# Attention and two MLPs on one core: normalising four units at their output, and masking eight on TensorE

## The chip, the cores and the metric

One core of a Trainium2 chip runs the whole kernel as one program. The metric is device time in microseconds, the median of the runs, lower is better. TensorE multiplies matrices (its weight loads are listed apart), VectorE and ScalarE do elementwise work, GpSimd does elementwise work that stays out of PSUM, and SyncE issues most transfers.

## The reference

For 4 batches, 8 heads, 576 positions and 64 columns per head: causal attention with a "forget" bias, then two MLPs over the 2304 rows of 512 columns.

```python
scores = scale * np.matmul(q, k.transpose(0, 1, 3, 2))
causal = np.triu(np.ones((S, S), dtype=bool), k=1)
cum = np.cumsum(np.maximum(s, 0.0), axis=-1)
bias = -(cum[:, :, :, None] - cum[:, :, None, :])
scores = np.where(causal, -1000000000.0, scores + np.minimum(bias, 0.0))
attn = np.exp(scores - np.max(scores, axis=-1, keepdims=True))
attn = attn / (np.sum(attn, axis=-1, keepdims=True) + 1e-09)
x = np.matmul(attn, v)            # heads side by side: (2304, 512)
h = np.maximum(x @ w_in, 0.0); x = (s * (h * h) + b) @ w_out          # first MLP
h = x @ w_in2; out = (np.maximum(h, 0.0) + alpha * np.minimum(h, 0.0)) @ w_out2
```

The weights arrive as 64-bit floats and are converted in the kernel.

## The kernel before

Attention is cut into 32 units. A unit is one batch, one pair of heads and one of two ranges of query rows: rows 0 to 320 in three blocks (64, 128 and 128 rows), or rows 320 to 576 in two blocks of 128. Units 0 to 3 are the first range of batch 0, units 4 to 7 its second range. `EARLY` is 4: these units have buffers of their own, in the room of weights that come later. `NATIVE` is 8: these units multiply in plain float32, the others in split halves.

For each head of a unit, `scores` first makes the bias of each block in an SBUF tile (L431 on ScalarE or L435 on VectorE) and has GpSimd put the mask on the diagonal square (`affine_select`, L439). TensorE multiplies queries and keys (L457); VectorE adds scores and bias and keeps the row extreme (L461); ScalarE takes the exponential with a running sum in `sm` (L473); VectorE adds 1e-9 and takes the reciprocal (L480, L481); GpSimd multiplies each block of probabilities by it (L484). `values` then transposes the probabilities on TensorE into two PSUM banks (L515), copies them out (L519), multiplies them with the values (L531) and copies the result into the MLP's input `xf` (L546). Heads follow each other as interleaved generators: `values` of one runs beside `scores` of a later one. Four PSUM buffers `b` serve scores and transposes, and single banks `hp`, `av` and `acc_first` the rest.

`busy` puts filler products of 512 bfloat16 columns (L97) into TensorE's queue in program order while the units 0 to 3 run. The first MLP works on blocks of 256 rows; its first block needs units 0 to 3, and its matmuls (L772 up, L886 down) are interleaved with later units at a pace set by `pace`. Weight packets are fetched on SyncE's queue and converted on ScalarE, VectorE and GpSimd (L140 to L142, L130, L131), four packets ahead. The order of instructions on each engine is not the written one: the program is built with `schedule_with_timeline_sim=True`, and a planner takes, for each engine, what is ready by its own costs, first written first. A tile's buffer is given out again when its last reader is done.

Of the kernel before, what the change touches and what calls it, by code (L numbers as in the profile page):

```python
# [8 lines left out]
F32 = mybir.dt.float32  # L9
# [10 lines left out]
def tile_forget_attention__then__two_mlps(  # L20
# [20 lines left out]
    nc = tc.nc  # L41
# [11 lines left out]
    R1 = IB[2][1]  # L53
    QK = S - R1 + S
    EARLY, NATIVE = NP, 2 * NP

# [20 lines left out]
    nc.sync.dma_start(out=gates, in_=s.rearrange("b h t -> (b h) t"))  # L79
    ident = const.tile([P, P], F32, name="ident")  # L80
    make_identity(nc, ident)
    misc = const.tile([P, 24], F32, name="misc")
    nc.vector.memset(misc[:, 23:24], 0.0)
    nc.scalar.activation(misc[:, 23:24], misc[:, 23:24], AF.Exp)
# [193 lines left out]
    class Unit:  # L278
        def __init__(self, n):
            self.n = n  # L280
            self.b, self.pr, self.rng = units[n]
            self.tag = "_".join(str(i) for i in units[n])
            self.h0 = 2 * self.pr
            self.blocks = (0, 1, 2) if self.rng == 0 else (3, 4)
            self.q0, self.q1 = (0, R1) if self.rng == 0 else (R1, S)
            self.nv = 3 if self.rng == 0 else 4
            self.probs = [None, None]

            self.early = 0 < n < EARLY
            self.native = n < NATIVE  # L290
            self.n_banks = 0
            self.cums = []
# [111 lines left out]
    def scores(u, h):  # L404

        own = HALF[h]
        head = u.b * H + u.h0 + h
        flip = u.native and h == 1
        nr = len(u.blocks)
        nm = two.tile([P, 3], F32, tag="nm", name=f"nm_{u.tag}_{h}")  # L410
        sm = two.tile([P, 3], F32, tag="sm", name=f"sm_{u.tag}_{h}")
        if u.rng == 0:
            nc.gpsimd.memset(sm[:, 0:1], 1.0)
        big = None if u.early else two.tile([P, 1088], F32, tag="probs", name=f"probs_{u.tag}_{h}")
        probs, col = {}, 0
        for r in u.blocks:
            i0, i1 = IB[r]
            rows = i1 - i0
            if u.early and r != 1:
                big, col = u.buf(two, 0, F32, "", f"probs{h}{r}"), 0  # L420

            width = -(-i1 // P) * P if i1 < S else S
            pt = probs[r] = big[:, col : col + width]
            col += width
            if width > i1:
                nc.gpsimd.memset(pt[:, i1:], 0.0)
            if r == 0:
                nc.gpsimd.memset(pt[64:P, 0:64], 0.0)

            if flip:  # L430
                nc.scalar.activation(  # L431
                    pt[:rows, :i1], u.cums[h][:rows, :i1], AF.Relu, scale=-1.0, bias=cumT[:rows, r, head : head + 1]
                )
            else:
                nc.vector.tensor_scalar(  # L435
                    out=pt[:rows, :i1], in0=u.cums[h][:rows, :i1], scalar1=cumT[:rows, r, head : head + 1],
                    scalar2=0.0, op0=ALU.subtract, op1=ALU.min,
                )
            nc.gpsimd.affine_select(  # L439
                out=pt[:rows, i0:i1], in_=pt[:rows, i0:i1], pattern=[[-1, rows]], base=0,  # L440
                channel_multiplier=1, compare_op=ALU.is_ge,
                fill=-MASKED if flip else MASKED,
            )
        u.probs[h] = probs
        for m, r in enumerate(u.blocks):
            i0, i1 = IB[r]
            rows, n = i1 - i0, i1
            a0 = i0 - u.q0
            pt = probs[r]
            init = -KEEP_ALL if flip else KEEP_ALL  # L450
            for j0, j1 in ([(0, n)] if n <= 512 else [(0, 320), (320, n)]):
                sc = u.bank("sc", f"sc{h}_{r}_{j0}")

                scr, all_ = sc[:rows, : j1 - j0], sc[:, : j1 - j0]
                aq = slice(a0, a0 + P)
                if u.native:
                    nc.tensor.matmul(all_, u.qk[0][own, aq], u.qk[1][own, j0:j1], start=True, stop=True)  # L457
                else:
                    nc.tensor.matmul(all_, u.xs[h][0][:, aq], u.xs[h][1][:, j0:j1], start=True, stop=False)  # L459
                    nc.tensor.matmul(all_, u.ql[h][:, aq], u.xs[h][1][:, j0:j1], start=False, stop=True)  # L460
                nc.vector.tensor_tensor_reduce(  # L461
                    out=pt[:rows, j0:j1], in0=scr, in1=pt[:rows, j0:j1], scale=SCALE if flip else -SCALE, scalar=init,
                    op0=ALU.subtract if flip else ALU.add, op1=ALU.max if flip else ALU.min,
                    accum_out=nm[:rows, m : m + 1],
                )
                if u.n < EARLY:
                    busy(1)
                init = nm[:rows, m : m + 1]
            if flip:
                nc.vector.tensor_scalar(  # L470
                    out=nm[:rows, m : m + 1], in0=nm[:rows, m : m + 1], scalar1=-1.0, scalar2=None, op0=ALU.mult
                )
            nc.scalar.activation(  # L473
                pt[:rows, :n], pt[:rows, :n], AF.Exp, bias=nm[:rows, m : m + 1], scale=1.0 if flip else -1.0,
                accum_out=sm[:rows, m : m + 1],
            )
            yield
        if u.n == 0:
            busy(4)
        nc.vector.tensor_scalar(out=sm[:, :nr], in0=sm[:, :nr], scalar1=1e-9, scalar2=None, op0=ALU.add)  # L480
        nc.vector.reciprocal(sm[:, :nr], sm[:, :nr])  # L481
        for m, r in enumerate(u.blocks):
            rows, n = IB[r][1] - IB[r][0], IB[r][1]
            nc.gpsimd.tensor_scalar(  # L484
                out=probs[r][:rows, :n], in0=probs[r][:rows, :n], scalar1=sm[:rows, m : m + 1],
                scalar2=1.0, op0=ALU.mult, op1=ALU.mult,
            )
        yield

    def values(u, h):  # L490
# [10 lines left out]
        for n_bank, bank in enumerate(banks):  # L501
            f0, fn = bank[0][1], bank[-1][1] + width[bank[-1][0]]
            tp = u.bank("tr", f"pt{h}_{n_bank}")
            moves = []
            for c, off in bank:
                for r in u.blocks:
                    i0, i1 = IB[r]
                    if P * c >= i1:
                        continue

                    partial = r and P * c > i0
                    o = off + i0 - max(q0, P * c)
                    moves.append((not partial, -c if partial else o, o, r, min(P * c, S - P)))
            for _, _, o, r, k0 in sorted(moves):
                nc.tensor.transpose(tp[:, o : o + P], u.probs[h][r][:, k0 : k0 + P], ident)  # L515
            n_p = (2 * h + n_bank) % 2
            if u.native:
                pf = two.tile([P, 512], F32, tag=("ph", "pl")[n_p], name=f"pf_{u.tag}_{h}_{n_bank}")
                (nc.scalar.copy, nc.vector.tensor_copy)[n_p](pf[:, f0:fn], tp[:, f0:fn])  # L519
                parts = (pf,)  # L520
            else:
                ph = two.tile([P, 512], F32R, tag="ph", name=f"ph_{u.tag}_{h}_{n_bank}")
                pl = two.tile([P, 512], F32R, tag="pl", name=f"pl_{u.tag}_{h}_{n_bank}")
                split(ph[:, f0:fn], pl[:, f0:fn], tp[:, f0:fn])
                parts = (ph, pl)
            yield
            for z, part in enumerate(parts):
                for c, o in bank:
                    w = width[c]
                    lhs = (u.vn if u.native else u.vs[h])[:, c].rearrange("p z d -> p (z d)")  # L530
                    nc.tensor.matmul(  # L531
                        av[:, nq - w : nq], lhs, part[:, o : o + w],
                        start=(c == 0 and z == 0), stop=(c == last_c and z == len(parts) - 1),
                        skip_group_check=True,
                    )
        if u.n < EARLY:
            busy(4 if (u.n, h) == (EARLY - 1, 0) else 1)
        t0 = u.b * S + q0
        while t0 < u.b * S + q1:
            t = t0 // T  # L540
            t1 = min((t + 1) * T, u.b * S + q1)
            a = t0 - u.b * S - q0
            cols = slice(a, a + t1 - t0)
            dst, src = x_block(t)[own, u.pr, t0 - t * T : t1 - t * T], av[own, cols]
            if u.native:
                nc.scalar.copy(dst, src)  # L546
            else:
                nc.scalar.copy(dst, av[HALF[1 - h], cols])
                nc.vector.tensor_tensor(out=dst, in0=src, in1=dst, op=ALU.add)
            t0 = t1  # L550
# [490 lines left out]
```

## Time and profile before

| | us |
|---|---|
| median of 3 runs | 1040.58 (1040.21 to 1042.25) |
| the profiled execution, its own time | 1043.1 |
| its span in the trace | 1041.2 |
| TensorE busy | 1021.4 (98% of the span) |
| VectorE, ScalarE, GpSimd busy | 686.3, 672.7, 468.1 |

Times are measured from the start of the span. The busy time of TensorE has modelled ends, so two of its instructions can overlap in the list; the distance from one start to the next is the safer measure. The granted clock is the share of 2.4 GHz that TensorE had.

### The profile page before, as it was taken

How to read it: one execution, taken by the hardware profiler on the slowest of the kernel's cores; microseconds unless marked ns; L12 is line 12 of the kernel's file. 1: busy time of each engine (PE TensorE's matmuls, PEld its weight loads, DVE VectorE, ACT ScalarE, POOL GpSimd, SP SyncE). 2: the span in 40 equal slices, each digit the busy share in tenths (PEclk: the TensorE clock that was granted, in tenths of full speed). 3: DMA queues.
4: the chain of work that ended last, by engine and by line, in shares of the span. 5: the costliest groups of instructions: out<-in, count | busy, mean ns of one | idle time of the engine just before them, and what ended most of it. 6: DMA issues, size and time to landing. Idle time of an engine off the chain costs nothing.

```text
span 1041.2 us, 20629 instructions
## 1 busy us (share of the span) xinstructions
PE 1021.4 (98%) x6952; PEld 927.0 (89%) x6952; DVE 686.3 (66%) x1605; ACT 672.7 (65%) x1669; POOL 468.1 (45%) x892
## 2 busy tenths in 40 slices
PE   9889999999999999999999999999999999999998
PEld 4568899999999999999999888998799999999996
DVE  6879875687677766667655975767775456446443
ACT  5868866777787877778776776645564455345443
POOL 5546675666677666677562100288721011001000
PEclk9889999999999999999999999999999999999999
DMA  7979533343232432234214762466654235334331
GB/s 157 268 174 252 150 63 69 69 97 72 52 84 62 90 92 52 67 68 93 64 44 145 241 201 81 124 194 200 196 178 143 98 101 179 105 95 132 107 104 55
DMA packets 197929, 125.44 MB, mean 120 GB/s; under 512 B 138496, under 2 KB 167936, under 8 KB 197824
## 3 DMA queue, kind: packets, MB, share of 16 engines
q1 hardware_dynamic: 193744, 123.56, 42.9%
q8 instruction: 55, 0.90, 0.4%
q10 hardware_dynamic: 4080, 0.57, 0.3%
q14 instruction: 50, 0.41, 0.1%
HBM read 106.19 MB, written 17.90 MB: 119 GB/s over the span
## 4 chain that ended last, share of the span: by engine, by line
PE 77%; DMA 5%; POOL 5%; ACT 4%; DVE 4%; issue 3%; SPq 1%; ACTq 0%; DVEq 0%; POOLq 0%
PE hp L772 18%; PE acc L896 16%; PE acc L886 16%; PE p L806 13%; PE pt L515 4%; PE av L531 4%; POOL sum L727 2%; PE sc L460 2%; DMA vn<-in_v_dram 1%; PE sc L459 1%; DMA sums_d<-w 1%; DMA wo<-in_moe_w_out_dram 1%; PE acc_first L97 1%; PE sc L457 1%; POOL probs L484 1%
## 5 line engine op out<-in xcount | busy, mean ns | idle before, releaser
L772 PE MATMUL hp<-xh,w 128*128 128x256 f32 (+1 forms) x1024 | 229.1, 301 | 0.5 <-ACT r L791 0.5
L896 PE MATMUL acc<-w,ring 128*128 128x512 f32 x864 | 214.1, 391 | 0.0
L896 PEld LDWEIGHTS acc<-w,ring 128*128 128x128 f32 x864 | 156.0, 188 | 27.8
L772 PEld LDWEIGHTS hp<-xh,w 128*128 128x128 f32 x1024 | 171.4, 189 | 6.6 <-ACT r L791 1.0
L886 PE MATMUL acc<-gh,w 128*128 128x256 f32 x896 | 172.3, 286 | 0.5 <-ACT res L915 0.3
L772 PE MATMUL hp<-xl,w 128*128 128x256 f32 (+1 forms) x512 | 152.6, 298 | 0.0
L886 PEld LDWEIGHTS acc<-gh,w 128*128 128x128 f32 x896 | 136.0, 189 | 3.1 <-issue 1.6
L872 POOL TENSOR_TENSOR cc<-u,t 128x256 f32<-128x256 f32 x32 | 25.9, 809 | 228.9 <-DVE u L863 198.9
L886 PE MATMUL acc<-gl,w 128*128 128x256 f32 x448 | 118.7, 288 | 2.0 <-POOL gl L131 2.0
L484 POOL TENSOR_SCALAR probs<-probs,sm 64x64 f32<-64x64 f32 (+4 forms) x160 | 91.0, 581 | 64.8 <-DVE sm L481 52.5
L473 ACT ACTIVATE probs<-probs,nm 64x64 f32<-64x64 f32 (+4 forms) x160 | 90.0, 563 | 37.8 <-DVE nm L461 25.7
L131 POOL TENSOR_TENSOR gl<-r,gh 128x256 fp32r<-128x256 f32 x112 | 89.3, 797 | 51.3 <-ACT gh L130 44.8
L806 PE MATMUL p<-xs,sums 128*128 128x256 f32 x768 | 104.4, 282 | 0.7 <-DVE u L848 0.7
L806 PEld LDWEIGHTS p<-xs,sums 128*128 128x128 f32 x768 | 97.8, 189 | 2.8 <-DVE u L848 1.2
L772 PEld LDWEIGHTS hp<-xl,w 128*128 128x128 f32 x512 | 97.1, 190 | 3.3 <-issue 0.4
L461 DVE CUSTOM_DVE_ANT_0 probs<-sc,probs 128x320 f32<-128x320 f32 (+3 forms) x160 | 68.2, 427 | 40.4 <-PE sc L460 28.0
L791 ACT ACTIVATE r<-hp 128x256 f32<-128x256 f32 (+1 forms) x144 | 58.1, 403 | 44.5 <-PE hp L772 36.9
L806 PEld LDWEIGHTS p<-xs,w 128*128 128x128 f32 x576 | 78.8, 189 | 9.0 <-DVE u L863 2.3
L806 PE MATMUL p<-xs,w 128*128 128x256 f32 x576 | 82.2, 283 | 2.4 <-DVE u L863 1.5
L886 PEld LDWEIGHTS acc<-gl,w 128*128 128x128 f32 x448 | 80.1, 189 | 4.8 <-POOL gl L131 2.6
L515 PE MATMUL pt<-ident,probs 128*128 128x128 f32 x480 | 75.0, 277 | 5.7 <-POOL probs L484 5.6
L817 DVE SCALAR_TENSOR_TENSOR ph<-pl,misc,ph 128x512 f32<-128x512 f32 x64 | 52.7, 823 | 38.2 <-ACT pl L833 38.0
(149 smaller groups left out, 2133.9 us busy)
## 6 DMA issues: line engine op xcount, KB each, us to landing
sums<-sums_d SPq DMA_DIRECT2D x128, 256.0 KB, 2.7
wi<-in_moe_w_in_dram SPq DMA_DIRECT2D x32, 512.0 KB, 5.0
wo<-in_moe_w_out_dram SPq DMA_DIRECT2D x32, 512.0 KB, 5.0
cum<-cum_d SPq DMA_DIRECT2D x32, 288.0 KB, 3.8
sums_d<-w SPq DMA_DIRECT2D x64, 128.0 KB, 1.9
cum<-cum_d SPq DMA_DIRECT2D x30, 160.0 KB, 3.2
nat<-in_k_dram SPq DMA_DIRECT2D x64, 72.0 KB, 2.5
x_d<-res SPq DMA_DIRECT2D x18, 256.0 KB, 2.2
```

The costliest lines, as they stand in the source:

```text
L131: lo_eng.tensor_tensor(out=lo, in0=src, in1=hi.bitcast(F32), op=ALU.subtract)
L461: nc.vector.tensor_tensor_reduce(out=pt[:rows, j0:j1], in0=scr, in1=pt[:rows, j0:j1], scale=SCALE if flip else -SCALE, scalar=init, op0=AL ...
L473: nc.scalar.activation(pt[:rows, :n], pt[:rows, :n], AF.Exp, bias=nm[:rows, m : m + 1], scale=1.0 if flip else -1.0, accum_out=sm[:rows, m ...
L484: nc.gpsimd.tensor_scalar(out=probs[r][:rows, :n], in0=probs[r][:rows, :n], scalar1=sm[:rows, m : m + 1], scalar2=1.0, op0=ALU.mult, op1=A ...
L515: nc.tensor.transpose(tp[:, o : o + P], u.probs[h][r][:, k0 : k0 + P], ident)
L531: nc.tensor.matmul(av[:, nq - w : nq], lhs, part[:, o : o + w], start=(c == 0 and z == 0), stop=(c == last_c and z == len(parts) - 1), ski ...
L772: nc.tensor.matmul(hs, a[:, c], b[c], start=(n == 0), stop=(n == len(terms) * NCC - 1))
L791: relus.append(nc.scalar.activation(r, hs, AF.Relu, scale=1.0 / W_SCALE).ins)
L806: nc.tensor.matmul(bank, lhs[:, c * P : (c + 1) * P], rhs[:, c], start=(start and c == 0 and z == 0), stop=(c == 1 and z == 2), skip_group ...
L817: nc.vector.scalar_tensor_tensor(out=r, in0=u, scalar=nalpha[:, f : f + 1], in1=r, op0=ALU.mult, op1=ALU.add).ins
L886: nc.tensor.matmul(banks[d] if count == 2 else acc[d // 2][:, d % 2], a[:, d * P : (d + 1) * P], b, start=(f == 0 and (d % 2 == 0 or count ...
L896: nc.tensor.matmul(banks[m], a[:, m * P : (m + 1) * P], b, start=(f == 0 and b is woh and a is gh), stop=(f == NF - 1 and a is gl),)
```

## The change

For units 0 to 3 (`LATE_SCALE`) the probabilities are not normalised. They are transposed and multiplied as the exponentials left them. The reciprocals of each block are then spread by TensorE over all partitions (a float32 product of a broadcast column with the identity) into the free end of the second transposed bank; ScalarE copies that spread into `xf`, where it had copied the result, and VectorE multiplies the result by it. For units 0 to 7 (`MASK_PE`) GpSimd's selection on the bias tile goes; TensorE adds the mask to the scores in PSUM, as one product of a bfloat16 identity with a bfloat16 mask for each block. Two constant tiles are made at the start.

```diff
+    LATE_SCALE = 4
+    MASK_PE = 8
...
+    one_mask = [const.tile([P, P], BF16, name=f"one_mask{z}") for z in range(2)]
+    causal = two.tile([P, T], F32, tag="r", name="causal")[:, :P]
+    nc.gpsimd.memset(causal, 0.0)
+    nc.gpsimd.affine_select(
+        out=causal, in_=causal, pattern=[[-1, P]], base=0, channel_multiplier=1, compare_op=ALU.is_ge, fill=MASKED
+    )
+    nc.scalar.copy(one_mask[0], ident)
+    nc.scalar.copy(one_mask[1], causal)
...
+            if u.n < MASK_PE:
+                continue
             nc.gpsimd.affine_select(
                 out=pt[:rows, i0:i1], in_=pt[:rows, i0:i1], pattern=[[-1, rows]], base=0,
...
                 if u.native:
+                    masked = u.n < MASK_PE and j1 == i1
                     nc.tensor.matmul(all_, u.qk[0][own, aq], u.qk[1][own, j0:j1], start=True, stop=True)
+                    if masked:
+                        nc.tensor.matmul(
+                            sc[:, i0 - j0 : i1 - j0], one_mask[0], one_mask[1][:, :rows], start=False, stop=True,
+                            skip_group_check=True,
+                        )
...
         nc.vector.reciprocal(sm[:, :nr], sm[:, :nr])
+        u.sums[h] = sm
         for m, r in enumerate(u.blocks):
+            if u.n < LATE_SCALE:
+                break
             rows, n = IB[r][1] - IB[r][0], IB[r][1]
             nc.gpsimd.tensor_scalar(
...
+        late = u.n < LATE_SCALE
+        if late:
+            spread = tp[:, 512 - nq :] if u.rng == 0 else u.bank("sc", f"spread{h}")[:, :nq]
+            for m, r in enumerate(u.blocks):
+                i0, i1 = IB[r]
+                nc.tensor.matmul(
+                    spread[:, i0 - q0 : i1 - q0],
+                    u.sums[h][: i1 - i0, m : m + 1].to_broadcast([i1 - i0, P]),
+                    ident[: i1 - i0, : i1 - i0], start=True, stop=True, skip_group_check=True,
+                )
...
-            if u.native:
+            if late:
+                nc.scalar.copy(dst, spread[own, cols])
+                nc.vector.tensor_tensor(out=dst, in0=src, in1=dst, op=ALU.mult)
+            elif u.native:
                 nc.scalar.copy(dst, src)
```

## Rows read from the trace of the kernel before

**Rows 1.** Busy us by stretch; then granted clock, DMA share, GB/s.

```profile
36.30:43.10 6.80, 6.80 (x19) 4.19 (x19) 5.35 (x18) 6.10 (x19) 3.00 (x7) 0.50 0.89 209
...
53.40:60.20 6.80, 4.50 (x14) 3.08 (x15) 4.59 (x15) 3.03 (x8) 5.49 (x9) 0.50 0.97 194
...
8.50:64.13 55.63, 49.58 (x203) 28.64 (x201) 44.84 (x154) 38.92 (x114) 29.44 (x68) 0.88 0.91 234
64.13:140.00 75.87, 74.57 (x498) 63.49 (x497) 67.45 (x139) 60.66 (x146) 49.81 (x73) 1.00 0.66 166
140.00:1041.00 901.00, 890.05 (x6235) 831.73 (x6233) 570.81 (x1307) 571.61 (x1409) 382.66 (x707) 1.00 0.39 110
```

**Rows 2.** Waits of TensorE, 8.50 to 64.13: us, times, longest.

```profile
PE pt L515 <- POOL probs L484: 4.9, 4, 2.8
```

**Rows 3.** TensorE in order of time: start, us, instruction.

```profile
33.12 1.05 PE L515 MATMUL pt<-ident,probs 128*128 128x128 f32 x6 [1.13 <-POOL probs L484]
...
55.70 0.90 PE L515 MATMUL pt<-ident,probs 128*128 128x128 f32 x3 [2.79 <-POOL probs L484]
...
64.13 0.47 PE L772 MATMUL hp<-xh,w 128*128 128x256 f32 x1
```

**Rows 4.** ScalarE in order of time.

```profile
10.15 0.35 ACT L473 ACTIVATE probs<-probs,nm 64x64 f32<-64x64 f32 x1 [7.47 <-DMA natk<-in_k_dram]
...
37.28 0.34 ACT L473 ACTIVATE probs<-probs,nm 64x64 f32<-64x64 f32 x1
...
40.46 0.55 ACT L473 ACTIVATE probs<-probs,nm 128x320 f32<-128x320 f32 x1
...
44.84 0.35 ACT L473 ACTIVATE probs<-probs,nm 64x64 f32<-64x64 f32 x1
...
49.02 0.19 ACT L473 ACTIVATION_READ_ACCUMULATOR probs<-probs,nm 128x1 f32 x1
```

**Rows 5.** VectorE in order of time.

```profile
32.95 0.90 DVE L141 TENSOR_SCALAR wt<-wt 128x512 uint32<-128x512 uint32 x1 [0.67 <-ACT wt L140]
...
39.50 0.42 DVE L141 TENSOR_SCALAR wt<-wt 128x512 uint32<-128x512 uint32 x1
...
41.52 0.40 DVE L131 TENSOR_TENSOR xl<-xf,xh 128x256 fp32r<-128x256 f32 x1
43.48 0.22 DVE L519 COPY pf<-pt 128x64 f32<-128x64 f32 x1 [1.56 <-PE pt L515]
...
53.54 0.25 DVE L480 TENSOR_SCALAR sm<-sm 128x3 f32<-128x3 f32 x1
...
54.30 0.16 DVE L481 RECIPROCAL sm<-sm 128x3 f32<-128x3 f32 x1
```

**Rows 6.** Busy time of GpSimd's line 484 in the first stretch.

```profile
8.50:64.13 55.63, 13.00 (x26) 0.88 0.91 234
```

**Rows 7.** TensorE in order of time: distances between starts.

```profile
9.20 0.59 PE L457 MATMUL sc<-turned 64*128 64x192 f32 x2
9.72 0.39 PE L97 MATMUL acc_first<-dense 128*128 128x512 bf16 x1
...
10.78 1.25 PE L97 MATMUL acc_first<-dense 128*128 128x512 bf16 x5
11.96 0.43 PE L457 MATMUL sc<-turned 64*128 64x64 f32 x2
...
15.99 0.82 PE L515 MATMUL pt<-ident,probs 128*128 128x128 f32 x6
16.74 0.59 PE L457 MATMUL sc<-turnedk,turnedq 64*128 64x192 f32 x2
...
26.07 0.33 PE L531 MATMUL av<-pf,vn 128*128 128x64 f32 x2
26.24 0.59 PE L97 MATMUL acc_first<-dense 128*128 128x512 bf16 x2
```

**Rows 8.** Busy time of GpSimd's line 439 in the first stretch.

```profile
8.50:64.13 55.63, 9.60 (x28) 0.88 0.91 234
```

More of the change, by code (lines that the diff above doesn't have):

```diff
@@ L287, in __init__ @@
             self.probs = [None, None]
+            self.sums = [None, None]
             self.early = 0 < n < EARLY
```

## The prediction

> **What bounds the kernel now.** I read the busy times by stretch first. From 140 us to the end TensorE is busy 890.05 of 901.00 us at the full clock, and from 64.13 to 140 it is busy 74.57 of 75.87 [rows 1]. Nothing else counts there: the kernel ends when TensorE has done its list. The first stretch is different. Between 8.50, where the first scores start, and 64.13, where the first MLP matmul starts (last row of [rows 3]), TensorE is busy 49.58 of 55.63 us, and its mean granted clock is 0.88 [rows 1]. So the time is a ledger of TensorE: its work, plus its idle time, plus what it loses at the low clock. The change can take from the last two in the first stretch only, and it adds to the first.
>
> What can be taken? The waits of TensorE in that stretch have one large entry: transposes of probabilities (L515) that waited for GpSimd's normalisation (L484), four times, 4.9 us together and 2.8 us the longest [rows 2]. The list of TensorE shows two: 1.13 us before the transpose at 33.12, and 2.79 before that at 55.70 [rows 3]. What lies behind the second is seen on three engines. ScalarE had the last exponential and its sum done at 49.02 + 0.19 = 49.2 [rows 4]; VectorE took up the sum only at 53.54, behind other work in its queue, and the reciprocal at 54.30 [rows 5]; GpSimd multiplied after that. The transpose could have run 6 us earlier had it needed only the exponentials.
>
> Then the clock. In 36.30 to 43.10 and 53.40 to 60.20 the granted clock is 0.50 (1.2 GHz) [rows 1]; the mean of 0.88 says that the rest of the stretch ran at 2.4 GHz (13.6 x 0.5 / 55.63 = 0.12). The first begins 3 us after the wait that ends at 33.12, the second inside the one that ends at 55.70 [rows 3]. TensorE is busy 6.80 us in the first and 4.50 us in the second; at the full clock the same work takes half of it, so 3.40 + 2.25 = 5.65 us are lost.
>
> **The change part by part.**
>
> *Normalisation of units 0 to 3.* GpSimd loses 24 of the 26 multiplications of L484, which take 13.00 us together [rows 6]. In their place the transposes follow the exponentials directly, and the 4.9 us of waits [rows 2] go. I take all 4.9, since each of the four waits names that line. The lower bound is 0, where the transpose then waits for something else just as late.
>
> *The clock.* If those waits go, I take it that both low stretches go: −5.65 us. The other end is 0: the clock falls somewhere all the same.
>
> *Spreads.* Per head three fp32 products of 64, 128 and 128 columns, 24 in all, each of two passes. Nothing like them is in the trace, so I bound them by start-to-start distances [rows 7]. Two passes of 64 columns inside a run of value products: 26.07 to 26.24, 0.17 us. Six one-pass transposes of 128 columns: 15.99 to 16.74, 0.125 each, hence 0.25 for two passes. A head is then 0.17 + 0.25 + 0.25 = 0.67 us, and eight heads 5.4 us. The upper end is a lone score product between fillers, two passes of 192 columns from 9.20 to 9.72: 0.52 x 24 = 12.5 us; the lower is the 64-column price for all, 0.17 x 24 = 4.1. I take 5.4, since the spreads stand in a row behind value products.
>
> *Masks on TensorE.* 40 bfloat16 products of 128 columns: 28 in the first stretch (24 of units 0 to 3, 4 of unit 4, whose scores run there), 12 after it. The filler of 512 columns in a run of five takes (11.96 − 10.78) / 5 = 0.236 us [rows 7]; a quarter is 0.06, so 40 x 0.06 = 2.4 us. The upper end adds what changing between kinds of product costs: the lone pair of 192 columns took 0.52, of which its columns at the transposes' rate are 0.125 x 1.5 x 2 = 0.375, so 0.145 for coming and going, and 40 x 0.205 = 8.2. I take 2.4, since the mask stands where a filler or another score product would have paid that change anyway. The Trainium skill, "TensorE: Matmul & The Clock Gate", section on the back-to-back issue gap, speaks against the cheap price: it gives some 81 ns for a matmul of 128 columns in a stream, which would make the masks 3.2 us and the whole sum 0.8 worse. The same section gives 131 ns for 512 columns, and there the trace has 236, so I keep to the row.
>
> *GpSimd's masks.* 28 selections of L439 take 9.60 us in the first stretch [rows 8]; all go there, and 12 later. No wait of TensorE in [rows 2] names them: 0. What hides them is that bias tiles are ready before the scores. One fill and one selection more at the start lie in GpSimd's first microseconds.
>
> *VectorE.* It gets 16 multiplications in place of nothing, 256 or 64 columns: by a subtraction of 256 columns at 41.52 (0.40) and a copy of 64 at 43.48 (0.22) [rows 5], 8 x 0.62 = 5.0 us. It gets back what GpSimd held up: the same 512-column shift takes 0.90 at 32.95 beside L484 and 0.42 at 39.50 without [rows 5]; one hit for each of eight groups is 8 x 0.48 = 3.8. Net +1.2, and VectorE is busy 44.84 of 55.63 there [rows 1]: taken as 0, and 1.2 if that room is gone. The last multiplication stands before the first MLP block: VectorE's 0.62 against what TensorE has left of unit 4 to transpose, 0.3 taken, 0 to 0.7.
>
> *ScalarE.* The 16 copies out of PSUM stay (another source). Two copies of 128 columns are new; each is under the 0.55 of a 320-column exponential, and ScalarE has nothing until 10.15, where it ends 7.47 us of waiting for a load [rows 4]: 0.
>
> *Waits that are added.* The tile of sums (`sm`, two buffers) lives until the spread has read it, so the exponentials of the head after next wait for the spread; behind them on ScalarE stand weight conversions. The transposed bank is held until ScalarE has copied the spread, and one bank (`hp`) serves every second transposition. I take 0, since the transposes come earlier by what L484 and its wait took; the price if not is a rival below.
>
> **Sum.** −4.9 − 5.65 + 5.4 + 2.4 + 0.3 = −2.45 us. The profiled execution took 1043.1 (span 1041.2), so 1040.65 in its own time. The median of the three runs is 1040.58, 2.5 under the profiled one; on that scale the forecast is 1038.1.
>
> **The rivals.** *(a) The clock is won back once only.* Another wait keeps one low stretch, some 2.8 us: −2.45 + 2.8 = +0.4, 1041.0. For it: TensorE has 6.05 idle us in the first stretch, and 1.1 of them are not L484's. Against: fillers cover most of it.
>
> *(b) The spread becomes the wait; slower.* Place: the exponentials of unit 3, first head, at 37.28 [rows 4]. They would need the spread of unit 2, first head, which follows the copy of its last transposed columns at 43.48 + 0.22 [rows 5] by 0.67: 44.4, so 7.1 us late if those transposes come no earlier. From the last of these exponentials (40.46 + 0.55) to the first of the second head (44.84) there are 3.8 us of slack, so 3.3 pass on, and the first low stretch stays (3.40): −2.45 + 3.3 + 3.4 = +4.3, 1044.8. It decides once that exponential starts later than about 41 on the old time scale. For it: the old order has that copy late. Against: it was late because of the wait for GpSimd and the low clock, which both stand before it.
>
> *(c) The products are dear.* At the upper ends: −10.55 + 12.5 + 8.2 + 0.3 = +10.45, 1051.0; half way from the forecast, +4.0, 1044.6. For it: before 29 us TensorE shows no gaps, so what is added there is paid in full.
>
> *(d) More is won than the ledger lists*, since the transposes come 6 us earlier in the last unit and the planner lays out the first stretch afresh: twice the forecast, −4.9, 1035.7.
>
> **How the numbers follow.** A change under 0.2% (2.1 us) can't be told from none here. The forecast case, with its own range from −4.5 to −0.5, has 0.47 (0.34 faster, 0.13 within); (a) 0.20 (within 0.18, slower 0.02); (b) 0.15 and (c) 0.10, all slower but 0.01; (d) 0.08, all faster. Faster 0.42, within 0.32, slower 0.26. The range leaves a tenth at each side: down to (d) and a little over it, up to (b) and the half-way (c): 1035 to 1045.
>
> **What would show it.** Right: no wait of TensorE for L484 before the first MLP matmul; granted clock 1.00 from 8.5 us on; that matmul at about 60.7 (64.13 − 4.9 − 5.65 + 5.4 + 28 x 0.06); spreads at 0.17 to 0.25 start to start; TensorE dense after it. Wrong: low stretches that stay or move; ScalarE's exponentials waiting for TensorE; spreads at 0.5 us; the first MLP block stopped by VectorE's multiplication or by weights, which would mean that the ledger of TensorE is not the whole time.

## The result and the profile after

The changed kernel takes 1046.37 us (median of 12 runs, 1044.22 to 1052.22), the kernel before 1040.74 beside it; the ratio is 1.0055, with a 95% interval of 1.0042 to 1.0067. The change costs 5.6 us. Forecast were 1038.1 and a range of 1035 to 1045, so the time lies above it.

Each run also tells its span and mean granted clock. TensorE at 1.2 GHz does half of what it does at 2.4 GHz: in the kernel before, four fillers in a row start 0.43 us apart at 41.05, where the granted clock is 0.50, and 0.22 us apart at 46.79, where it is 1.00.

```profile
41.05 1.91 PE L97 MATMUL acc_first<-dense 128*128 128x512 bf16 x4
...
46.79 1.03 PE L97 MATMUL acc_first<-dense 128*128 128x512 bf16 x4
```

So for a kernel in which TensorE is nearly always busy, span times mean clock is about the span that the run would have had at the full clock. It is used below as "span at full clock" (the clock has three digits, so one run is good to some 0.5 us). The medians, those of the kernel before from its largest set of runs, beside e9 to e12:

| | time | mean clock | span | span at full clock | time outside the span |
|---|---|---|---|---|---|
| before | 1040.87 (29 runs) | 0.996 | 1038.8 | 1034.0 | 1.98 |
| after | 1046.37 (12 runs) | 0.998 | 1043.7 | 1041.2 | 2.63 |

So the span at full clock, TensorE's list with its idle time, grew by 7.2 us, the clock gave back 2.3 (4.8 lost before, 2.5 after), and 0.65 lies outside the span. The three make the 5.6.

The profiled execution of the changed kernel is the slowest of its twelve (1052.22, mean clock 0.991). The rows by stretch, with the columns of [rows 1]:

```profile
11.00:21.20 10.20, 9.98 (x28) 4.39 (x28) 2.17 (x11) 2.04 (x8) 0.00 (x0) 0.50 0.69 175
8.50:68.60 60.10, 57.13 (x272) 34.78 (x277) 43.02 (x166) 39.47 (x115) 9.46 (x20) 0.91 0.84 220
68.60:140.00 71.40, 69.83 (x464) 59.23 (x462) 65.19 (x135) 58.23 (x137) 43.94 (x57) 0.98 0.65 171
140.00:1049.00 909.00, 896.73 (x6281) 838.76 (x6279) 571.82 (x1317) 574.01 (x1416) 387.04 (x711) 1.00 0.39 109
```

Against [rows 1] the first MLP matmul comes at 68.60 instead of 64.13, 4.5 us later. GpSimd is down from 29.44 to 9.46 us there, VectorE from 44.84 to 43.02. TensorE is busy 57.13 of 60.10 us. The two low stretches of before are gone; this execution has another at 11.0 to 21.2, where TensorE is busy 9.98 of 10.20 us. From the first MLP matmul to the end it takes 980.9 us instead of 977.1; two low stretches of 3.4 us, which cost half of their length, are nearly all of that.

The waits of TensorE in that stretch, which answer to [rows 2]:

```profile
PE sc L471 <- DVE sm L499: 1.6, 1, 1.6
PE pt L537 <- POOL probs L506: 0.6, 1, 0.6
PE sc L471 <- DVE turned L386: 0.5, 1, 0.5
PE acc_first L553 <- DVE pf L541: 0.3, 1, 0.3
PE acc_first L107 <- issue: 0.2, 1, 0.2
```

The 4.9 us for GpSimd's normalisation are gone (the 0.6 is unit 4, which still has it, at L506 now). Of other waits there are 2.6 us, where the kernel before had 1.1. The longest ends at 55.30. TensorE's list shows it, and masks and a head's spreads as well:

```profile
9.62 0.23 PE L473 MATMUL sc<-one_mask,one_mask 128*128 128x128 bf16 x1
9.69 0.38 PE L107 MATMUL acc_first<-dense 128*128 128x512 bf16 x1
...
40.66 1.07 PE L563 MATMUL pt<-ident,sm 64*128 64x64 f32 x6
41.56 0.59 PE L107 MATMUL acc_first<-dense 128*128 128x512 bf16 x2
...
52.50 1.25 PE L537 MATMUL pt<-ident,probs 128*128 128x128 f32 x10
55.30 1.02 PE L471 MATMUL sc<-turned 64*128 64x448 f32 x2 [1.55 <-DVE sm L499]
```

The mask at 9.62 costs 0.07 from start to start, where 0.06 was forecast. The six spread passes of a head cost 0.90 at 40.66, and 0.98 in the mean, where 0.67 was forecast. What the wait at 55.30 was for is seen on VectorE, whose list before it is:

```profile
53.76 0.54 DVE L579 TENSOR_TENSOR xf<-acc_first,xf 64x256 f32<-64x256 f32 x2
54.23 1.02 DVE L386 STREAM_TRANSPOSE turned<-nat 128x832 f32<-128x832 f32 x1
55.18 0.12 DVE L499 TENSOR_SCALAR sm<-sm 128x3 f32<-128x3 f32 x1
```

The view puts the wait down to L499, which ended last; the scores read nothing of it. The scores of unit 4 needed its turned queries and keys (L386, until 55.25), which stood behind two of the new multiplications (L579), and these behind weight conversions. VectorE's queue is what is late next.

And ScalarE shows the wait that rival (b) spoke of, an exponential that waits for a spread to release the tile of sums:

```profile
50.62 0.46 ACT L492 ACTIVATE probs<-probs,nm 128x192 f32<-128x192 f32 x1 [0.94 <-PE pt L563]
```

For a ledger of TensorE up to the first MLP matmul, each instruction is charged the distance to the next start, less the idle time between; half of what falls into a low stretch is put down to the clock (us, profiled executions):

| | fillers | scores | masks | transposes | spreads | values | other | idle | low clock | start | sum |
|---|---|---|---|---|---|---|---|---|---|---|---|
| before | 16.84 | 16.69 | 0 | 7.19 | 0 | 8.82 | 1.55 | 6.05 | 5.67 | 1.31 | 64.13 |
| after | 14.30 | 16.98 | 2.26 | 6.67 | 7.85 | 9.12 | 1.62 | 3.48 | 5.01 | 1.31 | 68.60 |

Not all of the 2.5 us less for fillers is real. The program has the same 59 in both kernels, but five are missing from the trace of the changed one, and their time is booked beside them. Another 0.7 us is the start: the last of the first sixteen fillers starts at 6.7 us in one execution and at 5.9 in the other. Up to 5.6 and 4.2 us they start 0.43 us apart, although the granted clock reads 1.00 there.

### The profile page after: what moved, and what is told of

Same layout as the page of the kernel before. It is cut to its first block, busy times and chain, and to the rows that moved or that the text cites. A ratio compares the mean times of both kernels' runs of the same rounds, so it can differ in the third digit from the quotient of the medians.

```text
span 1049.5 us, 20739 instructions
## 1 busy us (share of the span) xinstructions
PE 1030.4 (98%) x7035; PEld 935.8 (89%) x7040; DVE 683.5 (65%) x1621; ACT 673.8 (64%) x1671; POOL 447.5 (43%) x830
## 4 chain that ended last, share of the span: by engine, by line
PE 84%; DVE 4%; ACT 3%; DMA 3%; POOL 3%; issue 2%; SPq 0%; ACTq 0%; DVEq 0%; POOLq 0%
PE hp L807 20%; PE acc L921 18%; PE acc L931 17%; PE p L841 13%; PE av L553 5%; PE pt L537 4%; PE sc L471 2%; PE sc L479 2%; PE sc L478 2%; DMA sums_d<-w 1%; POOL sum L762 1%; PE acc_first L107 1%; DVE probs L446 1%; PE colsum L255 1%; DMA vn<-in_v_dram 1%
## 5 line engine op out<-in xcount | busy, mean ns | idle before, releaser
L492 ACT ACTIVATE probs<-probs,nm 128x192 f32<-128x192 f32 (+4 forms) x160 | 90.0, 562 | 42.5 <-DVE nm L480 23.5
L506 POOL TENSOR_SCALAR probs<-probs,sm 128x448 f32<-128x448 f32 (+4 forms) x136 | 79.9, 601 | 49.4 <-DVE sm L500 44.6
L826 ACT ACTIVATE r<-hp 128x256 f32<-128x256 f32 (+1 forms) x144 | 58.2, 404 | 46.5 <-PE hp L807 37.4
```

The source lines that it names most:

```text
L492: nc.scalar.activation(pt[:rows, :n], pt[:rows, :n], AF.Exp, bias=nm[:rows, m : m + 1], scale=1.0 if flip else -1.0, accum_out=sm[:rows, m ...
L506: nc.gpsimd.tensor_scalar(out=probs[r][:rows, :n], in0=probs[r][:rows, :n], scalar1=sm[:rows, m : m + 1], scalar2=1.0, op0=ALU.mult, op1=A ...
L826: relus.append(nc.scalar.activation(r, hs, AF.Relu, scale=1.0 / W_SCALE).ins)
```

## The experiments

Three theories. L: what is added to TensorE's list before the first MLP matmul is paid, and that is the loss. W: the late normalisation brings waits of its own. C: the low clock decides. From the second set on also P: the planner lays the program out anew at any edit, and that costs some us. The results stand together here; the ratio is to the kernel before on the same chip.

| | time | ratio, 95% interval | mean clock | span at full clock |
|---|---|---|---|---|
| e1, masks only | 1053.35 | 1.0120, 1.0100 to 1.0139 | 0.990 | 1040.5 |
| e2, late scaling only | 1049.46 | 1.0076, 1.0049 to 1.0103 | 0.993 | 1040.5 |
| e3, change, 8 buffers of sums | 1045.58 | 1.0040, 1.0017 to 1.0063 | 0.998 | 1040.5 |
| e4, before again | 1040.83 | 0.9995, 0.9977 to 1.0014 | 0.996 | 1034.3 |
| e5, change, spreads twice | 1058.04 | 1.0168, 1.0145 to 1.0190 | 0.996 | 1050.8 |
| e6, change, masks twice | 1053.64 | 1.0124, 1.0095 to 1.0153 | 0.994 | 1046.1 |
| e7, change, bfloat16 spreads | 1047.83 | 1.0081, 1.0055 to 1.0108 | 0.993 | 1039.3 |
| e8, change, 11 fillers less | 1055.83 | 1.0145, 1.0122 to 1.0167 | 0.991 | 1044.9 |
| e9, change, no normalising | 1041.48 | 0.9996, 0.9978 to 1.0014 | 0.995 | 1034.7 |
| e10, before, spreads unread | 1061.24 | 1.0200, 1.0166 to 1.0235 | 0.988 | 1046.9 |
| e11, before, 8 buffers of sums | 1047.05 | 1.0052, 1.0027 to 1.0077 | 0.990 | 1034.4 |
| e12, late for the last head only | 1047.34 | 1.0062, 1.0040 to 1.0084 | 0.995 | 1039.5 |
| e13, e9 and spreads unread | 1049.72 | 1.0087, 1.0065 to 1.0108 | 0.998 | 1045.1 |
| e14, e9 and multiplying | 1053.08 | 1.0119, 1.0100 to 1.0138 | 0.992 | 1041.7 |
| e15, ones beside v, no masks | 1065.00 | 1.0228, 1.0209 to 1.0247 | 0.984 | 1047.0 |
| e16, ones beside v and masks | 1062.92 | 1.0229, 1.0202 to 1.0256 | 0.982 | 1043.1 |
| e17, before, 3 buffers of sums | 1050.19 | 1.0093, 1.0078 to 1.0107 | 0.991 | 1037.3 |
| e18, before, 8 buffers of extremes | 1043.38 | 1.0024, 1.0007 to 1.0041 | 0.994 | 1034.9 |

**Parts, buffers and the clock (e1 to e4).**

```diff
-    LATE_SCALE = 4
+    LATE_SCALE = 0      (e1)
-    MASK_PE = 8
+    MASK_PE = 0         (e2)
-        sm = two.tile([P, 3], F32, tag="sm", name=f"sm_{u.tag}_{h}")
+        sm = two.tile([P, 3], F32, tag="sm", name=f"sm_{u.tag}_{h}", bufs=8)   (e3)
```

> Only the masks of units 0 to 7 move to TensorE; units 0 to 3 are normalised on GpSimd as before. Theory L (TensorE's list is full, so what is added to it is paid): 40 masks at the 0.06 to 0.07 us that they show start to start in the changed kernel are 2.4 to 2.8 us, so 1043.1 to 1043.6, and the waits for L484 stay. Theory W (the late scaling brings a wait of its own): no change, 1040.7 within 1. Theory C (the low clock decides): no change, 1040.7, or less if the clock stays up.

> Only the late normalisation of units 0 to 3; all masks stay on GpSimd. Theory L: the spreads cost 0.95 us a head, 7.6 in all, and the waits for L484 (4.9) go, so about 2.7 to 3.2 over the kernel before, 1043.4 to 1043.9. Theory W: all of the loss is here, 1046 or more. Theory C: as W if the clock stays down between 11 and 21 us, else about 1041.

> The whole change, with eight buffers for the tile of sums instead of two, so that no exponential waits for a spread. Theory L: as the changed kernel, 1046.4 within 1. Theory W: 3 us or more come back, 1043 or less. Theory C: as L.

> The kernel before, for the granted clock of each of its executions. Theory C, with the forecast's clock term: the mean clock is about 0.993 in most executions and the times lie near 1043 there. Theory L: most executions have a clock of 0.996 or more, so that the 5.65 us of low clock that the profiled execution showed were not there to be won in the median.

e3 goes against W as far as the tile of sums is concerned: without that wait the time is 0.8 us less than the change's, inside e3's interval. e4 settles the clock term: the kernel before has 0.995 or more in 10 of 12 runs, so the two long low stretches of its profiled execution were not the rule. The profiled execution of e4 has two of 3.4 us before the MLP, 3.41 lost, with nearly the same waits:

```profile
PE pt L515 <- POOL probs L484: 4.6, 4, 2.8
```

So one program with the same waits can lose half as much by the clock: the waits alone don't set the size of that loss. e1 and e2 fit no theory: each part alone costs more than both together (12 and 8 us), and each has a lower clock than either kernel. That raised P.

**Doses (e5 to e8).**

```diff
-            for m, r in enumerate(u.blocks):
+            for m, r in 2 * list(enumerate(u.blocks)):          (e5, spreads)
-                    if masked:
+                    for _ in range(2 * masked):                 (e6)
+            nc.gpsimd.tensor_scalar(out=hi, in0=sm, scalar1=1.0, scalar2=0.0, ...)   (e7, hi and lo bfloat16;
+            nc.gpsimd.tensor_tensor(out=lo, in0=sm, in1=hi, op=ALU.subtract)          two products with one_mask[0])
-        if u.n < EARLY:
-            busy(4 if (u.n, h) == (EARLY - 1, 0) else 1)        (e8)
```

> The whole change with every spread product issued twice (the second overwrites the first with the same numbers). Theory L (what is added to TensorE's list before the first MLP matmul is paid in full): 7.85 us more, as the 48 passes cost in the changed kernel's list, so 1054 within 2, and the first MLP matmul later by as much. Theory W (the spread's latency counts, not its work): a spread is 0.98 us longer, of which at most the last one shows, 1047 to 1048. Theory C (the low clock decides): no change in the mean clock and no more than 1 us.

> The whole change with every mask product issued twice (the masked scores are twice as low, their exponentials still 0). Theory L: 40 products more at 0.07 are 2.85 us, so 1049.2 within 1.5. Theory W: no change, 1046.4. Theory C: as W.

> The whole change with cheap spreads: the reciprocals are cut on GpSimd into a bfloat16 part and a bfloat16 rest, and spread by two bfloat16 products a block instead of a float32 product. Theory L: six products of about 0.06 a head, 0.36 instead of 0.98, so 5 us come back: 1041.4 within 1.5. Theory W: two GpSimd steps more lie before each spread, so as the changed kernel or up to 2 us slower. Theory C: no change if the mean clock stays at 0.998.

> The whole change without the 11 fillers that stand behind the values of units 0 to 3; the spreads are left in their place. Theory L: 11 fillers at 0.26 are 2.9 us, so 1043.5 within 1.5, if the clock stays up. Theory W: no change. Theory C: the fillers hold the clock, so the mean clock falls towards 0.99 and the time rises to 1050.

The second set of spreads costs 9.6 us at the full clock for 8.0 of list (15.86 instead of 7.85 in the ledger) and the second set of masks 4.9 for 2.0. So the list counts, as L says, and some 2 to 3 us come on top; both times lie above L's. e7 takes 4.1 us of list away (its 48 passes cost 0.079 each) and gets back 1.9 at the full clock, and loses that and more by the clock, 0.993 against 0.998. e8 fails L: without the 11 fillers (the traces show 45 instead of 54 before the first MLP matmul) the entry for fillers falls by only 0.75 us (13.55 instead of 14.30), idle time rose from 3.48 to 5.0, the clock fell to 0.991, and the time rose by 9.5. C foresaw the direction there, with 1050; 3.7 of the 9.5 are at the full clock.

**What the step is worth, and what a new plan is worth (e9 to e12).**

```diff
-        late = u.n < LATE_SCALE
-        if late: ...                                            (e9: no spread, result copied as before)
+        late = False
+            nc.tensor.matmul(spread[...], u.sums[h]...)         (e10: in the kernel before, all else as it was)
+        sm = two.tile(..., bufs=8)                              (e11: in the kernel before)
-            if u.n < LATE_SCALE:
+            if (u.n, h) == (LATE_SCALE - 1, 1):                 (e12: the break, and late; MASK_PE = 0)
```

> The whole change, but units 0 to 3 are not normalised at all: no spread, no multiplication at the output, ScalarE copies the result as before. It leaves out the division by the sums in those units. What the removed step alone is worth shows here. The forecast's terms: the waits (4.9) and the low clock (5.65) gone, masks 2.4 added, so 1040.8 - 8.2 = 1032.6. Theory L with what the changed kernel showed (idle time 2.4 less, clock 2 less, masks 2.85 more): 1040.8 - 1.6 = 1039.2. Theory P (the planner lays the stretch out anew at any edit, and that costs some us): 1042 to 1044.

> The kernel before, normalised on GpSimd and masked there, with the 24 spread products issued all the same into the free end of the transposed bank, where nothing reads them. Theory L: 7.85 us of list more, less what falls into idle time: 1046.5 to 1048.6. Theory W: they fall into the waits for L484, 1041 to 1043.

> The kernel before with eight buffers for the tile of sums: no instruction added or removed on TensorE, VectorE or ScalarE, only the plan laid out anew (half of the order rows of TensorE differ). Theory P: 2 to 5 us over the kernel before, 1043 to 1046. Theory L: no change, 1040.8 within 1.

> Only the last head of the first four units is normalised at its output, which is where the longest wait (2.79) stood; all else as before, masks on GpSimd. The forecast's terms: 2.8 of wait and 2.25 of low clock gone, 1 us of spread added, 1040.8 - 4 = 1036.8. Theory L with the shown terms: 1040.8 - 1.8 = 1039. Theory P: 1042 to 1045.

e9 asks most directly what the removed step is worth. With the masks on TensorE, with GpSimd's 24 multiplications gone and nothing in their place, the time is that of the kernel before; the forecast's terms gave 1032.6. If the masks cost their 2.85 us of list, taking the normalisation away is worth about as much. That is not settled: against e1, which has the same masks and normalises on GpSimd, e9 wins 12 us, 5.8 at the full clock. Against e9 the whole change, with spreads and multiplications, costs 4.9 us of time, 6.5 at the full clock. The waits of e9 show what took the place of [rows 2]:

```profile
PE av L553 <- ACT pf L541: 5.4, 2, 4.1
PE sc L471 <- DVE nm L480: 1.1, 1, 1.1
```

The 4.9 us are back as 5.4, at the next step: the value products wait for ScalarE's copy of the transposed probabilities. The first MLP matmul still comes at 61.13, 3 us earlier, with one low stretch of 3.4 us before it. e11 is the other surprise. Not an instruction of its arithmetic differs from the kernel before, and it costs 6.2 us, all by the clock: 1034.4 at the full clock against 1034.0. Its profiled execution, by stretch:

```profile
24.60:31.50 6.90, 6.90 (x19) 4.14 (x19) 2.04 (x12) 4.33 (x15) 4.93 (x16) 0.51 1.04 278
38.30:45.10 6.80, 6.80 (x22) 4.30 (x22) 4.01 (x22) 4.88 (x15) 1.25 (x4) 0.50 1.08 227
51.90:58.80 6.90, 6.55 (x15) 4.09 (x16) 6.90 (x17) 3.54 (x8) 3.93 (x8) 0.51 0.82 210
```

Three low stretches, where the kernel before had two. e12 was meant as the version that takes the longest wait and pays one spread; it costs 6.5 us, 5.5 at the full clock, for 1 us of list. e10 costs 20 us for 7.1 of list: 12.9 at the full clock, 7.5 by the clock. e10 and e12 lie above every theory.

**Spreads or multiplications, and sums for nothing (e13 to e16).**

```diff
+        if u.n < LATE_SCALE: (the spread products, read by nothing)                (e13, on e9)
+            nc.scalar.copy(dst, src)                                               (e14, on e9)
+            nc.vector.tensor_tensor(out=dst, in0=src, in1=dst, op=ALU.mult)
+            lhs = u.v3[c][:, h * D : (h + 2) * D]        # v of head 0, ones, v of head 1   (e15, e16)
+            nc.vector.reciprocal(dst, av[HALF[1 - h], cols])
+            nc.vector.tensor_tensor(out=dst, in0=src, in1=dst, op=ALU.mult)
```

> As the run without normalising, but the 24 spread products are issued and nothing reads them; ScalarE copies the result as before. It leaves out the division by the sums in units 0 to 3. Theory L: the loss is TensorE's list, so 1041.5 + 5 = 1046.5 within 2. Theory W: without the multiplication behind them nothing waits, 1041.5 to 1043.

> As the run without normalising, but the result is multiplied at the output by itself: ScalarE's copy and VectorE's 16 multiplications are there, the spreads are not. It squares the output of units 0 to 3 instead of dividing it. Theory L: VectorE's 5 us lie beside TensorE's list but for the last one, so 1041.5 to 1042.5. Theory W: 1045 or more.

> Masks on GpSimd as before; units 0 to 3 are normalised at the output without spreads: the half of the stationary value tile that belongs to the other head holds ones, so the unused half of the value product's output holds the sums, on all its partitions; VectorE takes their reciprocal out of PSUM and multiplies. Theory L: no product is added and the waits for L484 go, 1038 to 1040. Theory P: 1042 to 1047, by the plan that it gets.

> The same with the masks on TensorE for units 0 to 7. Theory L: 2.85 us over the one without those masks, so 1041 to 1043, and as the run without normalising. Theory P: anything from 1040 to 1047.

Against e9, the spreads alone cost 8.2 us and the multiplications alone 11.6 (10.4 and 7.0 at the full clock), both together 4.9 (6.5). Both times lie above L's, and e14 is where W has it (1045 or more). Two parts that come to 19.8 apart and 4.9 together can't be told apart by their times.

The traces tell more, if the place of the loss is asked for (one execution each; two executions of the kernel before, its own and e4's, differ by 1.8 us in the first measure). The first measure is the start of the first MLP matmul, less half of the low stretches before it. It is 57.3 and 59.1 us in the kernel before, 57.4 in e1, 59.4 in e9, 54.9 in e12, 56.8 in e14, and 55.6 to 58.2 in e11, e17 and e18. It is 61.8 or more in every version with all 24 spreads: e7 61.8, e13 62.2, e2 63.2, e3 63.4, the change 63.5, e8 63.8, e6 64.7, e10 66.1, e5 70.4. So the spreads make the first MLP matmul late, and the multiplications without them don't. The second measure is the way from that matmul to the end. In the kernel before, the change, e1, e12 and e14 it is:

```profile
64.13:1041.20 977.07, 964.61 (x6730) 895.22 (x6728) 638.26 (x1446) 632.27 (x1554) 432.47 (x780) 1.00 0.41 114
68.60:1049.50 980.90, 966.55 (x6742) 897.99 (x6740) 637.02 (x1451) 632.24 (x1552) 430.98 (x768) 1.00 0.41 114
65.92:1050.90 984.98, 967.17 (x6739) 896.96 (x6738) 638.23 (x1446) 632.75 (x1553) 431.08 (x768) 1.00 0.41 113
66.80:1052.40 985.60, 968.94 (x6743) 897.39 (x6742) 640.04 (x1456) 633.32 (x1556) 435.48 (x780) 1.00 0.41 113
61.89:1052.80 990.91, 971.00 (x6754) 900.53 (x6753) 640.28 (x1456) 635.40 (x1556) 430.00 (x768) 1.00 0.41 114
```

There e1, e12 and e14 lose most, although e12 adds no product behind that matmul, and e1 and e14 only masks that the change has there too (a few products of unit 4 have moved behind it). TensorE is idle 12.5 us in this part of the kernel before (5 us after its last product included), 14.4 with the change, and 17.8, 16.7 and 19.9 in the three. One wait that grows is that for GpSimd's normalisation of the later units, which no version touches: 0.7 us before, 0.9 with the change, then 1.9, 3.7 and 5.0, and 2.4 to 3.4 in e11, e17 and e18.

e15 and e16 pay a price of their own, seen in e15's rows by shape for VectorE (busy us, mean ns):

```profile
L576 DVE RECIPROCAL xf<-acc_first 64x256 f32<-64x256 f32 x4 | 7.0, 1759 | 0.8 <-PE acc_first L560 0.7
L576 DVE RECIPROCAL xf<-av 64x256 f32<-64x256 f32 x3 | 5.3, 1752 | 0.1
```

A reciprocal of 256 columns takes 1.76 us, so the sums that were free on TensorE cost VectorE some 16 us. How much of the loss of 24 and 22 us that makes is not shown.

**The scatter of the plan (e17, e18).** Both are the kernel before with another count of buffers: `bufs=3` on `sm`, `bufs=8` on `nm`.

> The kernel before with three buffers for the tile of sums; no instruction is added or removed. Theory P: 3 to 7 us over the kernel before, with a lower granted clock. Theory L: no change, 1040.8 within 1.

> The kernel before with eight buffers for the tile of row extremes; no instruction is added or removed, and the plan changes less than by the buffers of the sums (a fifth of the differing order rows). Theory P: 1 to 6 us over the kernel before. Theory L: no change, 1040.8 within 1.

Three edits of the kernel before that change no arithmetic cost 6.2, 9.7 and 2.9 us; at the full clock 0.4, 3.3 and 0.9. P holds in its sense, though e11 and e17 lost more than it had forecast (2 to 5 and 3 to 7): the kernel before has a plan that any new one is measured against, and most of what these three lose is low clock.

## Why the prediction was wrong

**The bound** held for the change. TensorE is dense from 140 us on, 896.73 of 909.00 us, and in the two profiled executions the changed kernel loses, at the full clock, some 6 us before the first MLP matmul and under 1 behind it. It did not hold for e1, e12 and e14. Of the signs of a right forecast three failed: the first MLP matmul came at 68.60 instead of 60.7, a pair of spread passes cost 0.33 instead of at most 0.25, and there is a low stretch after 8.5 us. Of the signs of a wrong one two came: a low stretch that moved, and an exponential that waits for TensorE.

**The waits (−4.9) failed.** That GpSimd's line would go was right. That nothing would stand in its place was not: TensorE's idle time before the first MLP matmul went from 6.05 to 3.48, so 2.6 came back. In e9, with still less in the way, none did. The prediction named the lower bound, a transpose that waits for something else just as late, and gave it no weight in the sum. VectorE's term was put at nothing, too, and its queue, with the new multiplications in it, is what the longest new wait (1.55 us) stands behind.

**The clock (−5.65) failed by its size.** Both low stretches went from the profiled execution, though another of 10.2 us came, and the change has the higher clock of the two kernels. But the term was read off one execution, and the 2.5 us by which that execution lay over the median were carried as a constant although they were part of the same loss. Over the runs the kernel before loses 4.8 to the clock and the changed one 2.5, so 2.3 came back.

**The spreads (+5.4) were too cheap:** 7.85. A pair of passes costs 0.33 in the mean; neither the 64-column value pair (0.17) nor two transposes (0.25) was the right row. **The masks (+2.4)** were right, at 2.85, and so were the two prices of **VectorE's** multiplication (0.43 and 0.21 measured). The three terms that failed come to 2.3 + 3.4 + 2.45 = 8.1 of the error of 8.3 us. That they close so well is partly luck: they are taken from the ledger of one execution and from the clock of many, and smaller entries are left out (masks +0.45, outside the span +0.65, behind the first MLP matmul some +0.7, the last multiplication, the fillers).

**The rivals.** No one of them gives the result; (b), at 1044.8, and (c), half way, at 1044.6, came nearest in time. Of (c) the spreads are about a third of the way to their upper end and the masks under a tenth. (b) had the right mechanism, seen on ScalarE, and the wrong weight: e3 takes it away and wins nothing that can be told. (a) had the clock nearly right: 2.3 of 5.65 came back, where it has 2.8 stay; its time, 1041.0, fails by the other terms. (d) did not happen. A mask of 128 columns costs 0.07, and the quarter of a filler, 0.06, is below that. The Trainium skill, "TensorE: Matmul & The Clock Gate", section on the back-to-back issue gap, which the prediction weighed, has some 81 ns for a product of 128 columns in a stream, above the 0.07 measured.

**What is shown and what is not.** Shown: without spreads and multiplications the change costs nothing (e9), more spreads or masks cost more (e5, e6), and every version with all the spreads reaches the first MLP matmul later than those without. At the full clock the change's 7.2 us lie above what three plans without any change of arithmetic scatter (0.4 to 3.3), but e1 and e12, without or nearly without spreads, lose 6.5 and 5.5 there, behind the first MLP matmul. The change's 5.6 us of time lie within the scatter of those three plans (2.9 to 9.7), since it has a better clock than they. So a cost is there, but its size in this measurement is that cost and the luck of two plans. Not shown: how the time divides between spreads and multiplications, and why a plan gets more low clock, or more idle time behind the first MLP matmul, than another. No version of the study beats the kernel before.

## What to carry to other kernels

A wait that is taken off one engine is won only if nothing else is as late: before a wait is counted as gain, look up when the next input of the waiting instruction is ready. A loss by the clock is read from many runs, never from the one that was profiled. And where a planner lays the program out, run an edit that changes nothing beside the one that is meant: here it moved the time by 3 to 10 us, more than most terms of the sum.

## What the runs showed that was not expected

A reciprocal on VectorE costs 6.9 ns a column (1.76 us for 256 columns of 64 partitions), a multiplication of the same tiles 1.7 (0.43 us). In a spread, a float32 pass of 64 columns cost no less than one of 128: 0.18 and 0.16 us in the mean, about twice a 64-column value pass (0.17 a pair). And TensorE's list shows hardly a gap in some of the low stretches (busy 9.98 of 10.20 us in the changed kernel, 6.90 of 6.90 in e11).
